# Attention, mixture of experts and feed-forward on one Trainium2 core: two-pass scores for the second pair of heads

## The chip, the core and the metric

The kernel runs on one core of a Trainium2 chip. The metric is the device time of one execution in microseconds (us), the median of several runs. PE is TensorE, ACT is ScalarE, DVE is VectorE, POOL is GpSimd, SP is SyncE, whose queue issues most of the DMAs here.

## The reference, cut to what matters

Three layers follow each other: causal attention with a bias from a cumulative sum, a top-1 mixture of experts on its output, and a feed-forward layer with a squared ReLU. The change touches the attention's scores only.

```python
batch, n_heads, seq, head_dim = (4, 8, 576, 64)      # q, k, v; s is (4, 8, 576)

scores = scale * np.matmul(q, k.transpose(0, 1, 3, 2))
causal = np.triu(np.ones((S, S), dtype=bool), k=1)
cum = np.cumsum(np.maximum(s, 0.0), axis=-1)
bias = -(cum[:, :, :, None] - cum[:, :, None, :])
scores = np.where(causal, -1000000000.0, scores + np.minimum(bias, 0.0))
...
attn = attn / (np.sum(attn, axis=-1, keepdims=True) + 1e-09)
return np.matmul(attn, v).astype(np.float32)
```

The output of all heads, as (2304, 512) rows, goes through `_moe_ref` (8 experts, 512 to 1024 to 512) and `_moe2_ref` (512 to 2048 to 512).

## The kernel before, in words

Attention works on 16 pairs of heads, pair `pp` = 0 to 15. A pair is cut into seven units of score rows (`order=[0, 1, 3, 11, 2, 10, 4]`): units 0 and 1 hold rows of both heads, 3 and 2 of the first head, 11 and 10 of the second, and 4 the last rows of both, which is called the tail. Each unit goes through the steps S (score matmuls, `emit_s`, line 636), M (mask and row minimum on DVE, line 663), E (exponential on ACT, line 680), T (transposes on PE, line 696) and V (copies out of PSUM, lines 715 and 717); later the product with v (line 733) and the transposes of the result (line 771) follow. S(1,0) below is step S of unit 0 of pair 1.

The order on every engine's queue is written out by hand. `at(key, fn, ...)` puts a step in a list, and the list is issued in the order of its keys; equal keys in the order of entry. One unit counts 1.0, so a pair counts 7, and pair `pp` has the keys around `7 * pp`. S of a pair's first unit stands at `7 * pp - 2.85`, so S(1,0) at 4.15 and S(2,0) at 11.15. An engine works through its own part of that order and waits at each instruction until its operands are there. SP's DMA issues are part of the same order.

q and k come as float32 and are split, after their transposes, in a high and a low part, each a float32r number for PE. For every pair, `qk_pe` transposes q (part 0), k (part 1) and the last 64 rows of both (part 2) on PE (lines 549 and 551) into a PSUM bank of the "t" ring, which has three banks and is shared with step T and the products with v; `qk_hi` copies the high part out on ACT (line 576), and `qk_lo` writes the low part with DVE (line 580). They go into the tiles `st_a` (three of them, used in turn) and `st_b` (two), each 128 partitions by 4 planes by 576: q high, k high, q low, k low.

The scores of a pair come in one of two forms:
- Direct, for pairs below `ND` (2 before): q of the two heads is kept in `sta` and `stb` with zeros in the other 64 partitions, and a block of scores is summed over four matmuls: q high by k high, q high by k low, q low by k high, and the bias from `cum_q` by `cum_k`.
- Packed, for the others: head 0 has both halves of `sta`, head 1 both halves of `stb`, so that one matmul contracts two products at once, and two matmuls do. This needs four more transfers, all issued by SP: `load_aug` (line 539) loads the extra rows of the bias from `aug_d` in DRAM into `stb` and `sta`; `spread_b` moves head 1's operands within the core into `stb[0:64]`, and `spread_a` moves head 0's into `sta[64:128]` (both line 584). POOL copies the other half for `stb` in `copy_b` (line 597) and clears a plane of `sta` (line 598).

`spread_b` reads `sta[64:128, 0:2]`, `copy_b` all of `sta[64:128]`; `spread_a` writes planes 0 and 3 of `sta[64:128]`. Every step whose operands overlap with an earlier one's waits for it.

The prologue (lines 1108 to 1197) builds the masks, the cumulative sums, `cum_q` and `cum_k`, writes `aug_d` (lines 1191 to 1195), and splits pair 0. `init_rest` (key 0.3, line 1206) has small DVE instructions (lines 1209 to 1218) and four small loads of the routing weights `wp` on SP (line 1221); `init_spare` (line 1225) clears tiles that take `cum_q`'s place. The loads of q and k of pair 4 have the key 3.01, v of pair 2 3.59. After attention the experts and the feed-forward layer follow on the same core.

The lines that the steps below come back to are `ND` (117), `qk_aps` (553), `move` (583), `emit_s` (609), the memsets (1161 to 1168), the products for `cum_q` (1179 to 1186), `init_spare`'s key (1236), and the keys of pair 1 (1247 to 1263).

Of the kernel before, what the change touches and what calls it, by code (L numbers as in the profile page):

```python
# [12 lines left out]
F32 = mybir.dt.float32  # L13
# [5 lines left out]
AF = mybir.ActivationFunctionType  # L19
ALU = mybir.AluOpType  # L20
# [9 lines left out]
K_ = dict(  # L30
    S=3,
    O=0,
    pbufs=4,
    NO=5,
    od=[-1.86, -0.33],
    lorder=[0, 2, 11, 10, 3, 1, 4],
    lvact=[[0], [1], [0], [1], [1], [0], [1, 0]],
    lpv=[[7.65, 7.66], [4.06, 5.56, 6.05, 6.9, 7.45]],
# [17 lines left out]
    qk=[-3.45, -2.16, -1.89],  # L56
    qkh=0.61,
    qkl=0.65,
    dup=-2.9,
    dupa=0.6,  # L60
# [22 lines left out]
    xt0=2.2,  # L83
    xt1=1.3,
    hv=0.9,
    q1=4.32,
)


# [1 line left out]
def attention_moe_ffn_kernel(  # L91
# [14 lines left out]
    nc = tc.nc  # L106
# [7 lines left out]
    SP = NB * P  # L114
    HP = H // 2
    NPAIR = B * HP
    ND = 2
    NO = K_['NO']
    MC = NT // P
    CAPS = [352, 320, 304, 304, 288, 288, 272, 256]  # L120
# [6 lines left out]
    scale = 1.0 / float(D) ** 0.5  # L127
# [89 lines left out]
    def at(key, fn, *args):  # L217
        tasks.append((key, len(tasks), fn, args))
# [232 lines left out]
    with tc.manual_schedule():  # L451
        with ExitStack() as actx:
# [16 lines left out]
            st_a = [(apool if a else apool0).tile([P, 4, S], F32R, name=f"sta{a}") for a in range(3)]  # L469
            st_b = [(apool if a else apool0).tile([P, 4, S], F32R, name=f"stb{a}") for a in range(2)]  # L470
# [15 lines left out]
            cum_q = cq_p.tile([P, 2 * ND, S], F32R, tag="cq", name="cum_q")  # L486
# [621 lines left out]
            with tc.tile_pool(name="prep", bufs=1) as prep:  # L1108
# [6 lines left out]
                cum_r = prep.tile([P, S], F32R, name="cum_r")  # L1115
                sel = prep.tile([P, 2 * ND], F32, name="sel")
# [11 lines left out]
                    out=mf, in_=zf[:, 0:P], pattern=[[-1, P]], compare_op=ALU.is_ge, fill=NEG, base=0,  # L1128
# [3 lines left out]
                    out=mt, in_=of[:, 0:P], pattern=[[1, P]], compare_op=ALU.is_gt, fill=0.0, base=0,  # L1132
# [7 lines left out]
                for hd in range(2):  # L1140
                    r = slice(64 * hd, 64 * hd + 64)
                    nc.scalar.copy(out=mask_t[r, S - TAIL:S], in_=mf[r, 64 * hd:64 * hd + 64])
                nc.vector.tensor_reduce(
                    out=sel.unsqueeze(2), in_=ident.rearrange("p (g r) -> p r g", r=NH)[:, 0:2 * ND], axis=AX.X, op=ALU.add)
                nc.vector.tensor_scalar(out=sq, in0=sq, scalar1=0.0, scalar2=None, op0=ALU.max)
                nc.vector.tensor_tensor_scan(
                    out=cum, data0=cum_r[0:NH].bitcast(F32), data1=sq, initial=0.0, op0=ALU.mult, op1=ALU.add)
# [4 lines left out]
                    out=cum_k[NH:2 * NH], in0=cum, in1=cum_k[0:NH].bitcast(F32), op=ALU.subtract)  # L1152
# [6 lines left out]
                for a in range(2):  # L1159
                    nc.gpsimd.memset(rs_t[a], 1.0)  # L1160
                for a in range(2):
                    nc.gpsimd.memset(st_b[a][0:64, 1].bitcast(F32), 0.0)
                nc.gpsimd.memset(carry, 0.0)
                nc.gpsimd.memset(carryb, 0.0)
                nc.gpsimd.memset(tbl, 0.0)
                nc.gpsimd.memset(wp, 0.0)
                nc.gpsimd.memset(st_a[1][64:128, 0:3:2].bitcast(F32), 0.0)
                nc.gpsimd.memset(st_b[1][0:64, 0:3:2].bitcast(F32), 0.0)
                load_qk(1)
                load_v(0)  # L1170
                for part in range(3):
# [5 lines left out]
                        qk_lo(0, part)  # L1177
                qk_lo(0, 2)
                for r in range(2 * ND):
                    if r < ND:  # L1180
                        nc.scalar.activation(
                            out=cum_q[:, r], in_=cum_r.bitcast(F32), func=AF.Copy, scale=sel[:, r:r + 1])
                    else:
                        nc.gpsimd.tensor_scalar(
                            out=cum_q[:, r], in0=cum_r.bitcast(F32), scalar1=sel[:, r:r + 1], scalar2=None,
                            op0=ALU.mult)
                nc.scalar.copy(out=tri, in_=mt)
                nc.scalar.copy(out=iota_r, in_=ii)
                nc.scalar.copy(out=iota8, in_=ii[:, 0:E])
# [3 lines left out]
                    out=aug_d[1, 0:2].rearrange("c r t -> (c r) t"), in_=cum_r[0:2 * NH].bitcast(F32))  # L1193
# [41 lines left out]
            NU = len(order)  # L1235
            at(NU * ND + 0.5, init_spare)

            def early(pp):
                return min(NU, 3 * max(pp - ND, 0))

            for pp in range(NPAIR):
                base = NU * pp
                t0 = base - NU
                if pp >= 2:
                    at(max(t0 + K_["ldqk"] - early(pp), t0 - 2 * NU + K_["scq"] - early(pp - 2) + 0.2), load_qk, pp)
                    at(t0 + K_["ldv"], load_v, pp)
                if pp >= 1:
                    if pp >= ND:
                        at(t0 + K_["sck"] - early(pp), scale_tail, pp, nc.gpsimd)
                    else:  # L1250
                        at(K_["od"][0], scale_tail, pp, nc.vector)
                    for part in range(3):
                        tq = t0 + K_["qk"][part] - early(pp) + (0 if pp >= ND else K_["q1"])
                        at(tq, qk_pe, pp, part)
                        at(tq + K_["qkh"], qk_hi, pp, part)
                        at(tq + K_["qkl"], qk_lo, pp, part)
                if pp >= ND:
                    tb = t0 + max(K_["dup"], K_["qk"][2] + K_["qkl"] - early(pp) + 0.4)
                    at(tb - 0.05, load_aug, pp, 1)
                    at(tb - 0.04, copy_b, pp)  # L1260
                    at(tb, spread_b, pp)
                    at(tb - K_["dup"] + K_["dupa"], spread_a, pp)
                    at(tb - K_["dup"] + K_["dupa"], load_aug, pp, 0)
                end = pp == NPAIR - 1
                units, vact, pv = (K_["l" * end + nm] for nm in ("order", "vact", "pv"))
                for i, un in enumerate(units):
                    u = base + i
                    at(u - K_["LS"], emit_s, pp, un)
                    at(u - K_["LM"], emit_m, pp, un)
                    at(u - K_["LE"], emit_e, pp, un)  # L1270
                    at(u, emit_t, pp, un)
                    at(u + K_["LV"], emit_v, pp, un, vact[i])
                for half in (1, 0) if end else (0, 1):
                    for jb, tv in enumerate(pv[half]):
                        at(base + tv, emit_pv, pp, half, [jb])
                    tv = base + pv[half][-1]
                    tx = tv + K_["xe"]
                    at(tv + K_["ov"], emit_ov, pp, half, K_["ovact"][half])
                    at(tv + K_["rc"], emit_rc, pp, half)
                    at(tv + K_["xt"], emit_xt, pp, half)  # L1280
                    if end:
                        at(tx, emit_xl, pp, half)
                    at(tx + 0.001, emit_xe, pp, half)
                    if end:
                        at(tx + 0.002, store_x, pp, *((0, 2) if half == 0 else (2, NB - 1)))
                        if half == 1:
                            at(tx + 0.002, store_x, pp, NB - 1, NB)
                if end:
                    for hd in range(2):
                        for half in range(2):  # L1290
                            at(tx + 0.003, emit_xa, pp, half, hd)
                else:
                    at(tv + K_["sx"], store_x, pp, 0, NB - 1)
                    at(tv + K_["sx"], store_x, pp, NB - 1, NB)
# [418 lines left out]
        else:  # L1713
            for i, job in enumerate(half_jobs(E + 1, "a") + half_jobs(E + 1, "b")):
                ta = 3.5 + 3.0 * i
# [108 lines left out]
```

## Time and profile before

| | us |
|---|---|
| median of 3 runs | 861.82 |
| lowest and highest | 861.45 and 862.03 |
| the profiled execution, its own time | 862.74 |
| its span, first to last instruction | 861.0 |

The profile is of one execution, taken by the hardware profiler. The span starts with the first instruction. A view by windows gives the busy time of each engine in a stretch of it, with the number of instructions in brackets, the granted TensorE clock (1.00 is 2.4 GHz, 0.50 is 1.2 GHz), the DMA engines' busy share and their rate. A timeline gives instructions in order of start, with the idle time of the engine before them in square brackets and what ended it. "PEld" is PE's weight load, which runs beside its matmuls; SPq is SP's queue, where a row is the time that issuing a DMA takes, not its transfer.

### The profile page before, as it was taken

The numbers are of one execution on the slowest core, as the hardware profiler recorded it, in microseconds if no ns is written. First come the engines' busy times: TensorE is split into PE (matmuls) and PEld (weight loads), VectorE is DVE, ScalarE is ACT, GpSimd is POOL, SyncE is SP. The second block draws the span as 40 slices with busy tenths as digits, with TensorE's granted clock in tenths as the row PEclk, the third lists the DMA queues.
The fourth block names the chain that finished last, engine by engine and source line by source line (L and its number), as shares of the span: only waits on it lengthen the run. The fifth ranks groups of instructions, "written<-read, shape, count | busy, mean of one in ns | idle before, by whom it ended". The sixth has DMA issues, their size and how long they took to land.

```text
span 861.0 us, 15161 instructions
## 1 busy us (share of the span) xinstructions
PE 843.1 (98%) x5412; PEld 748.7 (87%) x5412; DVE 520.4 (60%) x1180; ACT 452.3 (53%) x1012; POOL 262.1 (30%) x304
## 2 busy tenths in 40 slices
PE   8999999999999999999999999999999999999995
PEld 6876777777799999999999999999999999999994
DVE  7667777978777677768976767664233343232221
ACT  7787878988465446566655545443233232233221
POOL 6322334543126465566422232331101011001001
PEclk9999999999999999999999999999999999999999
DMA  7676677753287898999983433321010121001001
GB/s 168 137 162 142 144 183 180 178 127 91 78 278 232 255 252 266 233 280 274 296 246 96 147 120 101 100 84 62 13 62 37 37 75 38 1 1 37 1 0 40
DMA packets 113029, 113.14 MB, mean 131 GB/s; under 512 B 66034, under 2 KB 83954, under 8 KB 112947
## 3 DMA queue, kind: packets, MB, share of 16 engines
q1 hardware_dynamic: 104962, 96.68, 42.1%
q0 software_dynamic: 3664, 9.62, 3.3%
q10 hardware_dynamic: 4320, 5.80, 2.0%
q8 instruction: 45, 0.74, 0.4%
q14 instruction: 38, 0.30, 0.1%
HBM read 80.50 MB, written 23.32 MB: 121 GB/s over the span
## 4 chain that ended last, share of the span: by engine, by line
PE 47%; issue 31%; DVE 6%; ACT 6%; POOL 5%; DMA 4%; POOLq 1%; SPq 0%; ACTq 0%; DVEq 0%
PE z L1431 14%; PE z L1482 7%; PE z L1473 6%; PE s L636 5%; PE t L733 5%; PE t L696 4%; DMA cv<-in_moe_w_out_dram 2%; ACT p L680 2%; POOL out_dram L1541 1%; DVE w L250 1%; POOL cvm L1400 1%; PE t L549 1%; POOL cvm L1399 1%; ACT sta L576 1%; DMA w_out_d<-cvm 1%
## 5 line engine op out<-in xcount | busy, mean ns | idle before, releaser
L1431 PE MATMUL z<-xt,w 128*128 128x384 f32 (+6 forms) x1920 | 329.7, 320 | 0.7 <-DVE h L1442 0.6
L1431 PEld LDWEIGHTS z<-xt,w 128*128 128x128 f32 x1920 | 308.1, 188 | 9.8 <-DVE h L1442 1.2
L1482 PE MATMUL z<-w,h 128*128 128x512 f32 x864 | 214.9, 393 | 0.0
L1482 PEld LDWEIGHTS z<-w,h 128*128 128x128 f32 x864 | 160.7, 188 | 29.3
L1451 DVE SCALAR_TENSOR_TENSOR r<-z,r 128x384 f32<-128x384 f32 x96 | 53.3, 556 | 127.2 <-ACT r L1450 127.2
L1450 ACT ACTIVATE r<-z 128x384 f32<-128x384 f32 x96 | 47.2, 492 | 150.3 <-PE z L1431 149.3
L1473 PE MATMUL z<-h,w 128*128 128x304 f32 (+5 forms) x768 | 111.3, 294 | 0.4 <-DVE h L1442 0.2
L1473 PEld LDWEIGHTS z<-h,w 128*128 128x128 f32 x768 | 104.0, 189 | 1.2 <-ACT h L1441 0.4
L1399 POOL TENSOR_TENSOR cvm<-cvm,cva 128x512 f32<-128x512 f32 x32 | 43.5, 1361 | 170.6 <-DVE cva L1395 121.9
L1541 POOL DMA_INDIRECT out_dram<-ysb,tok_m x18 | 17.4, 969 | 245.5 <-ACT ysb L1528 183.2
L1458 DVE TENSOR_TENSOR h<-r,h 128x384 fp32r<-128x384 f32 x96 | 61.0, 636 | 50.3 <-ACT h L1457 49.7
L680 ACT ACTIVATE p<-p,nm 128x128 f32<-128x128 f32 (+3 forms) x144 | 84.3, 590 | 3.7 <-DVE nm L663 2.3
L1457 ACT CAST h<-r 128x384 fp32r<-128x384 f32 x96 | 49.3, 513 | 64.1 <-DVE r L1451 63.8
L250 DVE TENSOR_TENSOR w<-stg,w 128x1024 fp32r<-128x1024 f32 x49 | 75.1, 1534 | 5.4 <-ACT w L246 5.4
L663 DVE CUSTOM_DVE_ANT_0 p<-s,mask 128x128 f32<-128x128 f32 (+3 forms) x128 | 59.7, 486 | 30.4 <-PE s L636 29.3
L696 PE MATMUL t<-ident,p 128*128 128x128 f32 x400 | 69.1, 283 | 2.8 <-DVE sta L580 1.1
L246 ACT CAST w<-stg 128x1024 fp32r<-128x1024 f32 x49 | 51.4, 1049 | 22.0 <-POOL cvm L1400 18.2
L696 PEld LDWEIGHTS t<-ident,p 128*128 128x128 f32 x400 | 44.4, 140 | 18.7 <-ACT p L680 6.2
L597 POOL CAST stb<-sta 64x1152 fp32r<-64x1152 f32 x28 | 31.4, 1150 | 79.7 <-PE s L636 46.3
L1400 POOL TENSOR_TENSOR cvm<-cvs,cvm 128x512 f32<-128x512 f32 x32 | 54.2, 1694 | 2.5
L636 PE MATMUL s<-sta 128*64 128x288 f32 (+4 forms) x204 | 50.0, 342 | 0.9 <-DVE sta L580 0.9
L715 ACT COPY pt<-t 128x512 f32<-128x512 f32 (+1 forms) x94 | 47.0, 515 | 7.3 <-PE t L733 4.1
(242 smaller groups left out, 1024.8 us busy)
## 6 DMA issues: line engine op xcount, KB each, us to landing
stg<-in_moe_w_dram SPq DMA_DIRECT2D x42, 512.0 KB
cv<-in_moe_w_out_dram SPq DMA_DIRECT2D x16, 512.0 KB
stx<-in_moe_w_dram SPq DMA_DIRECT2D x14, 512.0 KB
cv<-in_moe_w_in_dram SPq DMA_DIRECT2D x14, 512.0 KB
xr<-yT_d SPq DMA_DIRECT2D x8, 768.0 KB
qk<-in_q_dram SPq DMA_DIRECT2D x32, 128.0 KB
v<-in_v_dram SPq DMA_DIRECT2D x32, 128.0 KB
stg<-in_moe_w_dram SPq DMA_DIRECT2D x16, 256.0 KB
```

The lines of the kernel that those rows point to most:

```text
L250: nc.vector.tensor_tensor(out=lo, in0=raw.pop(job), in1=hi.bitcast(F32), op=ALU.subtract)
L636: nc.tensor.matmul(ps[0:mw, d0:d0 + nn], lhsT=ql[r, m0:m0 + mw], rhs=kl[r, c0:c0 + nn], start=(i == 0 and (tail or n == 0)), stop=(done an ...
L663: nc.vector.tensor_tensor_reduce(out=dst, in0=src, in1=msk, scale=-1.0, scalar=3.0e38, op0=ALU.add, op1=ALU.min, accum_out=nm[:, c:c + 1])
L680: nc.scalar.activation(out=pt[:, cs], in_=pt[:, cs], func=AF.Exp, scale=-1.0, bias=nm[:, c:c + 1], accum_out=rs[:, r:r + 1])
L696: nc.tensor.transpose(tp[:, i * P:(i + 1) * P], pt[:, j0:j0 + P], ident)
L1399: nc.gpsimd.tensor_tensor(out=m, in0=m, in1=a.bitcast(F32), op=ALU.mult)
L1400: nc.gpsimd.tensor_tensor(out=m, in0=sq, in1=m, op=ALU.add)
L1431: nc.tensor.matmul(ps[:, 0:n], lhsT=wa[:, zw, kk, fl * P:(fl + 1) * P], rhs=xt[:, zx, kk, 0:n], start=(i == 0), stop=(i == 3 * KD - 1))
L1451: nc.vector.scalar_tensor_tensor(out=gg, in0=ps[:, 0:TT], scalar=0.0, in1=gg, op0=ALU.max, op1=ALU.mult)
L1458: nc.vector.tensor_tensor(out=ht[:, 1], in0=gg, in1=ht[:, 0].bitcast(F32), op=ALU.subtract)
L1473: nc.tensor.matmul(y_acc[g][d][:, 0:n], lhsT=wb[:, zw, fl, d * P:(d + 1) * P], rhs=ht[:, zh, 0:n], start=(f == 0 and i == 0), stop=(f == n ...
L1482: nc.tensor.matmul(acc, lhsT=ht[:, zh, c * P:(c + 1) * P], rhs=wb[:, zw, fl, :], start=(first and i == 0), stop=(last and i == 2))
```

## The change

`ND` goes from 2 to 1: pair 1 takes the packed form. Its transposes and copies get sooner keys (`q1` from 4.32 to 3.1): q at -0.35 instead of 0.87, k at 0.94 instead of 2.16, the last rows at 1.21 instead of 2.43, each with its high part 0.61 and its low part 0.65 behind. The steps of the packing are added for pair 1: `load_aug` for `stb` at 1.86, `copy_b` at 1.87, `spread_b` at 1.91, `spread_a` and `load_aug` for `sta` at 1.93. `cum_q` has two planes instead of four, both written by ACT; the two on POOL go. Two memsets for pair 1's direct form go, and one grows from one plane to two. `init_spare` comes at 7.5 instead of 14.5. The keys of all later pairs stay.

```diff
-    q1=4.32,
+    q1=3.1,
...
-    ND = 2
+    ND = 1
...
-                    nc.gpsimd.memset(st_b[a][0:64, 1].bitcast(F32), 0.0)
+                    nc.gpsimd.memset(st_b[a][0:64, 1:2 + a].bitcast(F32), 0.0)
...
-                nc.gpsimd.memset(st_a[1][64:128, 0:3:2].bitcast(F32), 0.0)
-                nc.gpsimd.memset(st_b[1][0:64, 0:3:2].bitcast(F32), 0.0)
...
                 for r in range(2 * ND):
-                    if r < ND:
-                        nc.scalar.activation(
-                            out=cum_q[:, r], in_=cum_r.bitcast(F32), func=AF.Copy, scale=sel[:, r:r + 1])
-                    else:
-                        nc.gpsimd.tensor_scalar(
-                            out=cum_q[:, r], in0=cum_r.bitcast(F32), scalar1=sel[:, r:r + 1], scalar2=None,
-                            op0=ALU.mult)
+                    nc.scalar.activation(
+                        out=cum_q[:, r], in_=cum_r.bitcast(F32), func=AF.Copy, scale=sel[:, r:r + 1])
...
             def early(pp):
-                return min(NU, 3 * max(pp - ND, 0))
+                return min(NU, 3 * max(pp - 2, 0))
...
-                    if pp >= ND:
+                    if pp >= 2:
                         at(t0 + K_["sck"] - early(pp), scale_tail, pp, nc.gpsimd)
...
-                        tq = t0 + K_["qk"][part] - early(pp) + (0 if pp >= ND else K_["q1"])
+                        tq = t0 + K_["qk"][part] - early(pp) + (0 if pp >= 2 else K_["q1"])
...
                 if pp >= ND:
                     tb = t0 + max(K_["dup"], K_["qk"][2] + K_["qkl"] - early(pp) + 0.4)
+                    if pp == 1:
+                        tb = K_["qk"][2] + K_["q1"] + K_["qkl"] + 0.05
                     at(tb - 0.05, load_aug, pp, 1)
                     at(tb - 0.04, copy_b, pp)
                     at(tb, spread_b, pp)
-                    at(tb - K_["dup"] + K_["dupa"], spread_a, pp)
-                    at(tb - K_["dup"] + K_["dupa"], load_aug, pp, 0)
+                    ta = tb - K_["dup"] + K_["dupa"]
+                    if pp == 1:
+                        ta = tb + 0.02
+                    at(ta, spread_a, pp)
+                    at(ta, load_aug, pp, 0)
```

## Rows read from the trace of the kernel before

**Rows 1.** Page, part 1: busy us, share of the span, instructions of each engine.
```profile
PE 843.1 (98%) x5412; PEld 748.7 (87%) x5412; DVE 520.4 (60%) x1180; ACT 452.3 (53%) x1012; POOL 262.1 (30%) x304
```

**Rows 2.** Timeline of PE: first score matmuls of pairs 1 and 2.
```profile
24.05 0.34 PE L636 MATMUL s<-sta 128*128 128x192 f32 x1
...
39.38 0.34 PE L636 MATMUL s<-sta 128*128 128x192 f32 x1
```

**Rows 3.** Windows: pair 1, pair 2, then pair 1's two halves.
```profile
24.05:39.38 15.33, 15.33 (x124) 13.21 (x122) 9.64 (x33) 10.91 (x32) 5.59 (x6) 1.00 0.72 156
39.38:52.16 12.78, 12.00 (x98) 9.68 (x96) 8.61 (x31) 10.66 (x31) 3.23 (x5) 1.00 0.73 169
...
24.05:31.35 7.30, 7.30 (x56) 6.60 (x55) 5.85 (x22) 6.50 (x21) 3.35 (x4) 1.00 0.58 132
31.35:39.38 8.03, 8.03 (x69) 6.60 (x68) 3.80 (x12) 4.41 (x13) 2.24 (x2) 1.00 0.84 178
```
The columns are the stretch, its length, then PE, PEld, DVE, ACT and POOL busy, the clock, the DMA share and GB/s.

**Rows 4.** Windows of line 636 alone: PE and PEld busy; pair 1's halves, pair 2.
```profile
24.00:31.35 7.35, 5.52 (x28) 3.99 (x28) 1.00 0.58 131
31.35:39.30 7.95, 3.38 (x21) 2.76 (x20) 1.00 0.85 179
39.30:52.10 12.80, 5.30 (x24) 3.34 (x24) 1.00 0.73 168
```

**Rows 5.** Timeline of SP's queue, pair 2's four transfers and the last of pair 3.
```profile
22.14 0.61 SPq L1221 DMA_DIRECT2D wp<-n_moe_w_output_gate_dram  x1
22.85 1.98 SPq L512 DMA_DIRECT2D qk<-in_q_dram  x2
...
29.32 0.44 SPq L539 DMA_DIRECT2D stb<-aug_d  x1
29.86 0.64 SPq L584 DMA_DIRECT2D stb<-sta  x1
...
34.73 0.62 SPq L584 DMA_DIRECT2D sta<-sta  x1
35.39 0.49 SPq L539 DMA_DIRECT2D sta<-aug_d  x1
...
46.66 0.50 SPq L539 DMA_DIRECT2D sta<-aug_d  x1
```

**Rows 6.** DMA issues of the first 60 us: one move and its size.
```profile
stb<-sta SPq DMA_DIRECT2D x3, 288.0 KB
```

**Rows 7.** Windows behind pair 2's spread_b; the last number is the DMA rate in GB/s.
```profile
30.50:31.00 0.50, 0.50 (x6) 0.50 (x4) 0.40 (x4) 0.50 (x2) 0.30 (x1) 1.00 0.08 23
31.00:32.70 1.70, 1.70 (x13) 0.87 (x13) 1.23 (x4) 1.10 (x3) 0.00 (x0) 1.00 0.91 172
```

**Rows 8.** Timelines and chain of the prologue: two loads from issue to use.
```profile
0.81 0.40 SPq L1110 DMA_DIRECT2D sq<-in_s_dram  x1
...
3.05 0.99 DVE L1145 TENSOR_SCALAR sq<-sq 32x576 f32<-32x576 f32 x1 [0.26 <-DMA sq<-in_s_dram]
...
1.73 3.99 DMA qk<-in_q_dram
```

**Rows 9.** Timeline of POOL: pair 2's copy_b and the idle time before it.
```profile
27.31 2.24 POOL L597 CAST stb<-sta 64x1152 fp32r<-64x1152 f32 x2 [6.19 <-DVE sta L580]
```

**Rows 10.** Timelines of DVE and PE: init_rest's first, q's low part, T of unit 3.
```profile
15.55 0.67 DVE L1209 TENSOR_SCALAR tok<-ij 128x20 int32<-128x20 int32 x1
...
17.31 0.42 DVE L717 COPY pt<-t 128x256 f32<-128x256 f32 x1
...
18.25 0.68 DVE L580 SCALAR_TENSOR_TENSOR sta<-t,sta 64x512 fp32r<-64x512 f32 x1
...
17.88 0.52 PE L696 MATMUL t<-ident,p 128*128 128x128 f32 x3 [0.25 <-DVE pt L717]
```

**Rows 11.** Windows behind PE's last matmuls; the clock is the third number from the end.
```profile
852.00:853.00 1.00, 0.03 (x1) 0.00 (x0) 0.00 (x0) 0.69 (x1) 0.81 (x2) 1.00 0.52 197
857.00:858.00 1.00, 0.00 (x0) 0.00 (x0) 0.00 (x0) 0.00 (x0) 0.00 (x0) 0.50 0.00 0
```

## The prediction, on record before the changed kernel ran

> **What bounds the kernel now.** I read the page's busy shares first, then the windows around the second pair's scores, then SP's queue. TensorE (PE) is busy 98% of the span, the other engines 30 to 60% [rows 1], so time is won where PE loses work and lost where it is made to wait. The stretch that the change is about runs from the first score matmul of pair 1 at 24.05 to that of pair 2 at 39.38 [rows 2]: 15.33 us, PE busy in all of it; the next pair, with two passes, takes 12.78 us with PE busy 12.00 [rows 3]. The reader should see in these rows that pair 1 is bound by PE alone, and that in its first half ACT is nearly full too (6.50 of 7.30 us).
>
> The second thing to see is SP's queue, which issues the DMAs one after another [rows 5]. The last small load of the routing weights (wp) goes out at 22.14, the q and k of pair 4 from 22.85, and so on without a gap to pair 2's four transfers: its extra rows for stb at 29.32, the move into stb (spread_b) at 29.86, the move inside sta (spread_a) at 34.73, the extra rows for sta at 35.39. Pair 2's scores begin at 39.38. An early need of pair 1 meets a queue that is full of other issues.
>
> **What is removed.** Each direct pair issues 48 score matmuls, a packed one 24. Line 636 keeps PE busy 8.89 us in pair 1's stretch (5.52 in its first half, 3.38 in its second, which add up so but for rounding) and 5.30 in pair 2's [rows 4]. So 24 matmuls are worth 8.89 - 5.30 = 3.59 us of PE time, split as the rows split: 2.23 in the first half, 1.36 in the second. The second half has ACT busy only 4.41 of 8.03 us [rows 3], so there all 1.36 count. In the first half ACT has 6.50 us of work, of which the softmax of pair 0's tail (0.78) can run ahead, while PE waits; the half can then not be shorter than some 5.7 us, which leaves 7.30 - 5.7 = 1.6 of the 2.23. I take 1.36 + 1.6 = 2.9 us, with ends 3.59 (PE alone counts) and 15.33 - 12.78 = 2.55 (pair 1 gets pair 2's period).
>
> **What is added, with one answer each.** On POOL the two products for cum_q and two memsets go, one memset doubles, and copy_b for pair 1 comes, like that of pair 2 (2.24 us) [rows 9]. POOL waited 6.19 us ahead of that one, so I cost this at nothing; without the cover copy_b would be 2.24 us later. ACT and DVE lose copies, since q's two 64-row halves become one 128-row copy: DVE has one 0.68 us instruction fewer for q's main part [rows 10], and three small ones become one. This lies in the prologue, ahead of the wait below, and I count nothing for it. init_spare's memset goes out one pair sooner, on a POOL that idles: nothing.
>
> **What is moved, and what it waits for.** Pair 1's first transposes stand at unit -0.35 now, ahead of T(0,0). The low part's subtract for q stands at 0.29999..., just ahead of init_rest at 0.3, which keeps DVE from 15.55 to the first copy behind it, some 1.7 us; before, it stood behind it [rows 10]. The three transposes of pair 1 also hold the three "t" banks longer: T of unit 3 (17.88 before, [rows 10]) now needs the bank that pair 1's k frees only when DVE has done the low part of q (0.68), init_rest (1.7), a copy, a mask step and the low part of k. I estimate that at 20.4; the work from there to pair 1's scores is as before, so PE would come to S(1,0) at about 25.8 instead of 24.05. If nothing else held S(1,0), this would cost 0 to 1.7 us.
>
> Something else does. The packed scores need both moves and both loads of extra rows. Their places are units 1.86 to 1.93, behind wp (0.3) and ahead of pair 4's q and k (3.01). So on SP load_aug comes at 22.85, where pair 4's load stood, and spread_b 0.54 us behind it as in pair 2, at 23.39 [rows 5]. spread_a overwrites sta[64:128, 0], which spread_b reads, so it has to wait until spread_b has landed; in the kernel before 4.87 us of other issues lay between the two, and no row shows that wait. It queues up SP: pair 4's q and k, pair 2's v and pair 2's own transfers stand behind it.
>
> How long a move takes, no row says directly. Pair 2's spread_b went out at 29.86, the DMA engines moved 23 GB/s until 31.00, and then 172 GB/s for 1.70 us [rows 7], some 300 KB in all, about the 288 of the move [rows 6] and its 18 of extra rows: 2.8 us from issue to landing. The nearest rows on either side are the 72 KB load of s, issued at 0.81 and used by DVE at 3.05, that is 2.24 us, and the first q load, 3.99 us in the chain that ended last [rows 8]. I take 2.8, since it is the same transfer, and keep 2.24 and 3.99 as ends.
>
> The sum: spread_b 23.39 + 2.8 = 26.2, spread_a issued there, the extra rows 0.66 later (34.73 to 35.39) at 26.9, and these land 2.24 after issue: **29.1**. S(1,0) starts there instead of 24.05, 5.05 us later. PE stands from 25.8 to 29.1, and everything behind S(1,0) in its queue stands too. Then 15.33 - 2.9 = 12.4 us to S(2,0): 41.5. The other way to S(2,0) is SP: the last of pair 1's four issues is over at 27.4, 4.55 us behind 22.85, so pair 2's last one moves from 35.39 to 39.9, or to 38.7 if two long q issues of before (1.98 and 1.54 us instead of some 1.14, [rows 5] shows the first) don't come again. It lands at 41.0 to 42.2, the same as PE's 41.5. So S(2,0) is 41.5 - 39.38 = 2.1 us later. Pair 3's last transfer went out at 46.66 [rows 5], 5.4 us before the end of pair 2's stretch, so there SP has time to spare. I carry the 2.1 us to the end unchanged.
>
> The profiled execution took 862.74 us; its span is 861.0, and the median of the runs shown is 861.82, that is 0.92 below. The sum is a difference within this one trace, so I add it to the median: 861.82 + 2.1 = **863.9 us**. Its own bounds: with legs of 2.24 S(1,0) is at 28.6 and, with 3.59 won, S(2,0) at 40.3, 1.0 late; with 3.99 it is 32.1, and with 2.55 won 44.9, 5.5 late. That is 862.8 to 867.3.
>
> The Trainium skill (DMA: Bandwidth & Descriptors, Queues, rings and completion order) says that completion on an issuing queue isn't first in, first out, so a later DMA may write before an earlier one has finished. By that rule the wait between the moves is needed, and the forecast stands; if a queue kept order, spread_a could follow at once, and the time would be that of the second case below. No run here shows it yet.
>
> **The rivals.** *Back to back* (0.20): spread_a doesn't wait for spread_b. It goes out at 24.05, the extra rows at 24.7, landing at 26.95; S(1,0) is 2.9 late and wins 2.9: 861.8, or 861.1 with 3.59. For it: nothing in the code but one overlapping slice forces the wait. Against it: the slice does overlap.
>
> *Not late at all* (0.13), the other side: the four transfers land before PE gets to S(1,0), at 24.05 to 25.8. Then 2.9 to 3.59 are won less 0 to 1.7: 858.2 to 860.6, say 859.5. The point from which it decides is SP: load_aug would have to go out by 19.5 or so for 25.8 (6.25 us lie between 22.85 and 29.1), ahead of the wp loads, and the rows put it at 22.85. For it speaks that pairs 0 and 1 are short of PE time alone, and that a gap on PE lets ACT and DVE run ahead, so some of it could come back.
>
> *The gap costs the clock, or pair 2 stalls too* (0.12): the granted clock was 1.00 (2.4 GHz) while PE's last matmuls ended at 852, and 0.50 (1.2 GHz) at 857, with PE idle between [rows 11]. If that happened in the gap before S(1,0), pair 1's packed scores (5.30 us of PE time) would take up to twice as long: up to 5.3 us more, 864 to 869, say 867. Against it: the forecast gap is shorter than that idle stretch. The Trainium skill (TensorE: Matmul & The Clock Gate, What's actually happening) says that the throttled state is the default and activity releases it. By that rule PE would come out of a long gap at the low clock; the last rows agree, none within the kernel does.
>
> *No change* (0.05): the 2.9 us and the delay cancel elsewhere, for instance in pair 2's wait of PE of 0.78 us (its 12.78 against 12.00 busy): 861.8.
>
> **How the numbers follow.** The forecast has 0.50, the rivals 0.20, 0.13, 0.12 and 0.05. The likeliest case gives 863.9, with 862.8 to 867.3 as its own range. The range over all reaches down into the third case and up to the end of the first: 860.2 to 867.4. Less than 2 in 10 is outside, most of the third case and part of the fourth. A measurement of this kernel tells 0.2% (1.72 us) from no change, so faster means under 860.1 and slower over 863.54. Faster: most of the third case, 0.12, and 0.02 of the second, 0.14. Same: the second's 0.16, the fifth's 0.05, and 0.10 of the first, whose lower end lies under the limit, 0.31. Slower: the rest, 0.55.
>
> **What would show it.** In the changed kernel S(1,0) starts near 29, with PE idle some 3 us ahead of it and the last DMA into sta as its releaser; SP shows a wait of some 2.2 us between spread_b and spread_a; line 636 is busy near 5.3 us in pair 1's stretch, and the stretch is about 12.4 us; S(2,0) starts near 41.5. I am wrong if S(1,0) starts before 27, or if the periods from pair 2 on change by more than some tenths of a us.

## The result and the profile after

The changed kernel takes **868.73 us** (median of 4 runs, 867.54 to 869.95) against 861.92 of the kernel before (4 runs, 861.45 to 862.45): ratio 1.0079, interval 1.0061 to 1.0096. It is slower, by 6.8 us, where 2.1 were forecast; the sign is right, the size is not: the time lies 1.3 us above the upper end of the range. The profiled execution took 869.95 us, its span is 868.3 (before: 861.0).

Page, part 1, of the changed kernel (against [rows 1]):
```profile
PE 840.9 (97%) x5388; PEld 746.5 (86%) x5388; DVE 519.5 (60%) x1177; ACT 451.4 (52%) x1009; POOL 260.4 (30%) x303
```
PE has 24 matmuls and 2.2 us of busy time fewer, and the span is 7.3 us longer. So PE waits somewhere for more than it saved. Its timeline says where. The timeline of PE, changed kernel, at the first scores of pairs 1 and 2 (against [rows 2]; columns: start, length, what, and in brackets the idle time before and its releaser):
```profile
23.33 0.55 PE L696 MATMUL t<-ident,p 128*128 128x128 f32 x3
31.89 0.71 PE L636 MATMUL s<-sta 128*128 128x192 f32 x2 [8.01 <-DMA sta<-aug_d]
...
46.69 0.45 PE L636 MATMUL s<-sta 128*128 128x192 f32 x2
...
211.16 0.45 PE L636 MATMUL s<-sta 128*128 128x192 f32 x2
```
PE is ready at 23.88 and gets its operands at 31.89: an idle stretch of 8.01 us, ended by the last small load into sta. S(1,0) is 7.84 us later than before, S(2,0) 7.31 later. From S(2,0) on nothing is lost or won: to the first score of the last pair it is 211.16 - 46.69 = 164.47 us here and 164.44 before (39.38 to 203.82). The whole loss lies between 23.88 and 46.69.

SP's queue, changed kernel (against [rows 5]):
```profile
21.46 1.57 SPq L1214 DMA_DIRECT2D wp<-in_moe_w_gate_dram  x1
...
23.73 0.51 SPq L539 DMA_DIRECT2D stb<-aug_d  x1
24.33 0.63 SPq L584 DMA_DIRECT2D stb<-sta  x1
27.62 0.61 SPq L584 DMA_DIRECT2D sta<-sta  x1
28.32 0.45 SPq L539 DMA_DIRECT2D sta<-aug_d  x1
...
41.21 0.48 SPq L539 DMA_DIRECT2D sta<-aug_d  x1
```
The chain is the forecast one: spread_b, a wait of SP, spread_a, the extra rows, S(1,0). Its legs are longer than forecast: 3.29 us between the two moves and 3.57 us from the last issue to S(1,0). What the DMA engines did meanwhile is seen in the DMA view of 24 to 32 us, 40 slices of 0.2 us each (busy tenths, GB/s):
```profile
DMA  1023030089999982000000005999999759967975
GB/s 10 1 15 21 3 94 0 0 196 219 207 242 196 184 173 58 0 0 0 0 0 0 0 0 127 230 196 196 184 196 184 196 141 221 236 145 165 210 170 128
```
The data of spread_b run from 25.6, 1.3 us behind its issue, to about 27.2, and spread_a goes out 0.4 us after they end. Nothing moves from 27.2 to 28.8. The data of spread_a (288 KB at some 196 GB/s are 1.5 us) run from 28.8, and the last small load, issued at 28.32, shares the engines with them and with pair 4's q behind it. The trace's chain view of this stretch gives 3.23 us from issue to landing for spread_b and 3.43 us for that load.

Windows of the changed kernel: within the idle stretch, the end of the low clock (two rows), pair 1, pair 2 (against [rows 3]; the clock is the third number from the end):
```profile
28.00:29.00 1.00, 0.00 (x0) 0.00 (x0) 0.00 (x0) 0.00 (x0) 0.00 (x0) 0.50 0.11 25
...
37.00:38.00 1.00, 1.00 (x5) 0.70 (x4) 0.03 (x1) 1.00 (x5) 1.00 (x2) 0.50 0.98 208
38.00:39.00 1.00, 1.00 (x8) 0.86 (x7) 1.00 (x4) 0.71 (x3) 0.88 (x3) 0.97 0.98 191
...
31.89:46.69 14.80, 14.80 (x96) 12.50 (x97) 8.71 (x31) 9.92 (x29) 5.04 (x7) 0.79 0.70 154
46.69:59.47 12.78, 12.00 (x99) 9.68 (x97) 8.63 (x31) 10.66 (x31) 3.86 (x5) 1.00 0.68 157
```
Window of line 636 alone, pair 1 (against [rows 4]; PE and PEld busy, then the clock):
```profile
31.80:46.60 14.80, 6.78 (x24) 4.47 (x24) 0.79 0.69 153
```
While PE idles, the clock falls from 1.00 to 0.50 (2.4 to 1.2 GHz), and it stays there until 38, with PE at work again from 31.89. The 24 score matmuls take 6.78 us instead of the 5.30 that 24 take at full clock [rows 4]. So the changed pair 1 takes 14.80 us, hardly less than the 15.33 of before.

### The profile page after: what moved, and what is told of

It is laid out like the page before. It is cut to its first block, busy times and chain, and to the rows that moved or that the text cites. A ratio compares the mean times of both kernels' runs of the same rounds, so it can differ in the third digit from the quotient of the medians.

```text
span 868.3 us, 15110 instructions
## 1 busy us (share of the span) xinstructions
PE 840.9 (97%) x5388; PEld 746.5 (86%) x5388; DVE 519.5 (60%) x1177; ACT 451.4 (52%) x1009; POOL 260.4 (30%) x303
## 4 chain that ended last, share of the span: by engine, by line
PE 50%; issue 31%; DVE 6%; ACT 5%; POOL 4%; DMA 2%; POOLq 1%; SPq 0%; ACTq 0%; DVEq 0%
PE z L1429 17%; PE z L1471 9%; PE z L1480 7%; PE t L733 4%; PE s L636 4%; PE t L696 3%; ACT p L680 2%; POOL out_dram L1539 1%; PE t L549 1%; ACT sta L576 1%; POOL cvm L1398 1%; DVE w L250 1%; PE z L333 1%; PE z L1071 1%; PE z L1099 1%
## 5 line engine op out<-in xcount | busy, mean ns | idle before, releaser
L597 POOL CAST stb<-sta 64x1152 fp32r<-64x1152 f32 x30 | 33.7, 1151 | 87.6 <-PE s L636 51.2
```

## The experiments

The theory after the result: (a) S(1,0) waits for a chain of two dependent legs, a move and then a second move with a small load behind it, and the chain starts late behind a full SP queue; (b) the idle stretch costs the clock; (c) the saved matmuls win what was forecast. Rivals: the sooner transposes themselves do the harm; or the clock would be low here anyway. Ratios are against the kernel before on the same chip.

**e1, the sooner transposes alone.** In the kernel before, with its four passes:
```diff
-    q1=4.32,
+    q1=3.1,
```


> The kernel before with q1 = 3.1 alone: pair 1 stays at four passes, its transposes and copies come 1.22 units sooner. Theory 1 (the loss is the wait of S(1,0) for the two moves and the extra rows, and the clock that falls in it): the sooner transposes cost nothing, 861.3 to 862.5 us, S(1,0) within 0.5 us of 24.05. Rival (the new order of the prologue, with the low part of q ahead of init_rest and the PSUM banks held longer, is what costs): 864 us or more, S(1,0) at 25 or later.

862.07 us, ratio 1.0012 (1.0001 to 1.0022). Timeline of PE:
```profile
23.95 0.56 PE L636 MATMUL s<-sta 128*128 128x192 f32 x3
...
39.26 0.45 PE L636 MATMUL s<-sta 128*128 128x192 f32 x2
```
S(1,0) and S(2,0) come 0.10 and 0.12 us sooner than before. That edit is harmless to the stretch; the loss comes with the packing. The median is 0.8 us above the kernel before's all the same. The last pair starts 0.08 us sooner than before (203.74), so the 0.8 us lie behind the attention part; why stays open.

**e2, the wp loads taken out of SP's way.** In the changed kernel the four wp loads of init_rest become a step of their own behind pair 1's transfers:
```diff
+            def load_wp():
...
             at(0.3, init_rest)
+            at(2.5, load_wp)
```


> The changed kernel with the four small wp loads taken out of init_rest and issued at 2.5, behind pair 1's moves. They took SP from 20.15 to 23.69 us. Theory 1: SP is the one that is late, so load_aug goes out at about 20.2 and S(1,0) starts about 3.5 us sooner, near 28.4; PE's gap is some 4.5 us instead of 8.0. If the clock falls all the same, 865.2 us; if it holds at 2.4 GHz, about 862.8. Rival (the moves wait for their operands, not for SP): S(1,0) stays near 31.9 and the time at 868.7.

866.27 us, ratio 1.005 (1.0033 to 1.0067). Timelines of SP and PE:
```profile
20.67 0.70 SPq L584 DMA_DIRECT2D stb<-sta  x1
24.46 0.62 SPq L584 DMA_DIRECT2D sta<-sta  x1
25.17 0.45 SPq L539 DMA_DIRECT2D sta<-aug_d  x1
...
28.39 0.71 PE L636 MATMUL s<-sta 128*128 128x192 f32 x2 [6.11 <-DMA sta<-aug_d]
...
44.37 0.44 PE L636 MATMUL s<-sta 128*128 128x192 f32 x2 [2.03 <-DMA sta<-aug_d]
```
The chain starts 3.66 us sooner and S(1,0) 3.50 sooner. So SP's place in time does count. But the leg between the moves is 3.79 us, the idle stretch still 6.11, the clock at 0.50 from 25 to 32. And S(2,0) wins only 2.32: it now waits itself, for pair 2's last load, which goes out at 40.56, only 0.65 us sooner than in the changed kernel, since the wp loads now stand ahead of it on SP. Soon behind that wait of 2.03 us the clock is at 0.50 once more, from 46 to 49, and the last pair starts 5.86 us later than before (209.68).

**e3, the wait between the moves taken away.** For pair 1, spread_b reads pair 0's sta, so that spread_a overwrites nothing that is still read; head 1 of pair 1 gets pair 0's operands in one half:
```diff
             def spread_b(pp):
                 a, b = st_of(pp)
+                a = st_of(0)[0] if pp == 1 else a
```


> The changed kernel, but spread_b of pair 1 reads pair 0's sta, so spread_a no longer has to wait until spread_b has landed (head 1 of pair 1 gets pair 0's operands in one half, so its scores are others; the work is the same). Theory 1: spread_a goes out right behind spread_b, at about 25.0 instead of 27.6, S(1,0) starts near 29.3 and the time falls by 2.6 us or more: 866.1 if the clock still falls, 863.7 if it holds. Rival (the landing of the last transfers is set by traffic, not by when spread_a is issued): S(1,0) within 1 us of 31.9, 868 us or more.

867.22 us, ratio 1.0056 (1.0039 to 1.0073). Timelines of SP and PE:
```profile
24.41 0.61 SPq L584 DMA_DIRECT2D sta<-sta  x1
25.12 0.74 SPq L539 DMA_DIRECT2D sta<-aug_d  x1
...
29.31 0.71 PE L637 MATMUL s<-sta 128*128 128x192 f32 x2 [5.17 <-DMA sta<-aug_d]
```
spread_a follows 0.73 us behind spread_b (issued at 23.68) instead of 3.29, so the overlapping slice is what makes SP wait. S(1,0) is 2.58 us sooner; the last load now takes 4.19 us, with 576 KB of moves ahead of it instead of 288. The stretch of 5.17 us costs the clock all the same (0.50 until about 35), and the kernel is still 6.0 us slower than the one before on this chip.

**e4, PE kept busy in the gap.** 30 matmuls on constants, into the scores' bank, ahead of S(1,0):
```diff
+            at(4.149, warm, 30, 512, "s")
```


> The changed kernel with 30 matmuls on constants (128x512, bfloat16) right ahead of S(1,0), which keep PE busy for about 6.5 of the 8.0 us that it waits. Nothing else is changed. Theory 1: the clock stays at 2.4 GHz through pair 1's stretch, S(1,0) still starts near 31.9, the stretch shrinks from 14.8 to about 12.4 us and the time falls by 2.4: about 866.3 us. Rival (the low clock costs nothing, since ACT and DVE or the transfers set the pace of the stretch): 868.7 us, the stretch still 14 us or more.

866.73 us, ratio 1.0063 (1.0046 to 1.008). Timeline of PE, and the window of pair 1:
```profile
23.76 6.64 PE L500 MATMUL s<-onesb 128*128 128x512 bf16 x30
31.72 0.44 PE L636 MATMUL s<-sta 128*128 128x192 f32 x2 [1.32 <-DMA sta<-aug_d]
...
44.30 0.44 PE L636 MATMUL s<-sta 128*128 128x192 f32 x2
```
```profile
31.72:44.30 12.58, 12.53 (x97) 9.77 (x97) 8.88 (x32) 9.88 (x30) 5.33 (x7) 1.00 0.77 169
```
S(1,0) starts where it does in the changed kernel, the clock stays at 1.00, and the stretch takes 12.58 us instead of 14.80. This separates the two parts of the loss: the low clock costs **2.2 us**, and the saved matmuls are worth 15.33 - 12.58 = **2.75 us**. The Trainium skill (TensorE: Matmul & The Clock Gate, What's actually happening) says that the throttled state is the default and activity releases it; this pair of runs agrees, 0.79 mean clock in the stretch behind an idle gap, 1.00 behind a busy one. The loss at S(2,0) then splits into 7.84 late - 2.75 won + 2.2 clock = 7.3 us. That this meets the measured 7.31 is no further test, since both terms are taken from the same 12.58; what e4 adds is the split. At the last pair e4 is 2.39 us ahead of the changed kernel (208.77 against 211.16); in the medians less shows, 5.5 us over the kernel before against 6.8, and the two intervals overlap.

**e5, pair 1's transfers on POOL's queue.** The four DMAs go out from gpsimd instead of SP, spread_b ahead of copy_b:
```diff
-                move(a[64:128, 0::3, 0:S], a[0:64, 0:2, 0:S])
+                move(a[64:128, 0::3, 0:S], a[0:64, 0:2, 0:S], nc.gpsimd if pp == 1 else nc.sync)
...
-                    at(tb, spread_b, pp)
+                    at(tb - 0.045 * (pp == 1), spread_b, pp)
```


> The changed kernel with pair 1's four transfers issued by POOL instead of SP, spread_b ahead of copy_b; all else as changed. SP's queue is then as in the kernel before. Theory (SP is late for spread_b, and a move takes 3.3 us and the last load 3.6): spread_b goes out at about 19.6 when pair 1's high parts are done, spread_a at about 23, S(1,0) starts near 27.5, PE's gap is some 3.6 us and the clock holds; then the stretch takes 12.6 us, S(2,0) starts near 40.1 and the time is about 862.3 us. Rival (transfers from POOL's queue are slower than SP's by as much as the wait that they save): S(1,0) at 30 or later, 866 us or more.

864.97 us, ratio 1.004 (1.0025 to 1.0054), between the two cases expected. Timelines of POOL and PE:
```profile
20.13 0.64 POOL L584 DMA_DIRECT2D stb<-sta  x1 [2.28 <-ACT sta L576]
...
24.64 0.59 POOL L584 DMA_DIRECT2D sta<-sta  x1 [0.95 <-DMA stb<-sta]
...
29.71 0.71 PE L636 MATMUL s<-sta 128*128 128x192 f32 x2 [5.52 <-DMA sta<-aug_d]
```
spread_b goes out 4.2 us sooner, as soon as its operands are there (its releaser is ACT's last high part). But the legs are 4.51 and 4.49 us (the last load issued at 25.22), longer than SP's 3.29 and 3.57, so S(1,0) wins 2.2 us only and the gap still costs the clock. Why POOL's legs are longer was not separated: its own copy_b runs beside the first one, and SP, which no longer waits, has its own loads under way beside both (the DMA engines move 0.91 MB from the issue of the last load to its landing, and 0.55 MB in the changed kernel).

**e6, and the transposes sooner still.** e5 with
```diff
-    q1=3.1,
+    q1=1.5,
```


> As the run with POOL's queue, and pair 1's transposes another 1.6 units sooner (q1 = 1.5), where PE, ACT and DVE have gaps. Theory (the packing loses by its wait alone; where the transfers land before PE comes to S(1,0), the 24 matmuls are won): high parts done near 15, spread_a out near 19, the last load landed near 23.5, S(1,0) starts at 24 to 25 with a gap under 1 us, the stretch takes 12.6 us, S(2,0) starts at 36.6 to 37.6, and the time is 858.5 to 860.0 us, below the kernel before. Rival (the sooner transposes push pair 0's scores back, and the packed pair gains nothing where ACT and DVE bound it): S(2,0) at 39.4 or later, 861.3 us or more.

862.64 us, ratio 1.0019 (1.001 to 1.0029), a miss for the theory. The operands now arrive in time, and another loss appears ahead of them. Timelines of DVE, POOL and PE, and two windows:
```profile
17.06 1.17 DVE L1206 TENSOR_SCALAR ik<-ij 128x20 int32<-128x20 int32 x1
18.26 1.06 DVE L1207 TENSOR_SCALAR idab<-ik 128x20 bf16<-128x20 int32 x1
...
17.05 2.24 POOL L597 CAST stb<-sta 64x1152 fp32r<-64x1152 f32 x2
...
22.05 1.12 PE L696 MATMUL t<-ident,p 128*128 128x128 f32 x4 [2.91 <-ACT p L680]
...
29.06 0.45 PE L636 MATMUL s<-sta 128*128 128x192 f32 x2
...
41.36 0.45 PE L636 MATMUL s<-sta 128*128 128x192 f32 x2
```
```profile
21.00:22.00 1.00, 0.00 (x0) 0.00 (x0) 1.00 (x5) 0.82 (x3) 0.92 (x2) 0.67 1.06 248
22.00:23.00 1.00, 0.95 (x5) 0.95 (x6) 0.36 (x4) 1.00 (x3) 0.58 (x2) 0.50 0.86 189
```
S(1,0) has no wait left, and its stretch takes 12.30 us. But copy_b on POOL now runs beside init_rest on DVE, whose two small integer instructions take 1.17 and 1.06 us (0.20 and 0.23 in the changed kernel) and end when the two copies end, at 18.2 and 19.3. init_rest keeps DVE 3.4 us, the softmax of pair 0 is late, PE stands 2.91 us, and the clock is at 0.50 until 28. The Trainium skill (SBUF — State Buffer, SBUF: two separate sides) says that GpSimd and some kinds of DVE instruction take a shared port pair as an exclusive lock for a whole instruction; the coinciding ends agree with that, but no run here shows that these two are of such a kind.

**e7, DVE's part of init_rest out of the way.** e6 with these DVE instructions as a step within pair 1:
```diff
+            def init_ids():
...
             at(0.3, init_rest)
+            at(8.9, init_ids)
```


> As the run with POOL's queue and the sooner transposes, and init_rest's small DVE instructions (token numbers, 3.4 us there beside POOL's copies) go to the key 8.9. Theory (what was left of the loss there was PE's wait for DVE at 19.1 and the clock that fell in it, not the packing): no gap over 2 us before S(1,0), the clock holds, S(1,0) starts at 24 to 25.3 when the last load lands, the stretch takes 12.6 us, S(2,0) starts at 36.6 to 37.9, 858.4 to 859.7 us, below the kernel before. Rival (a packed pair 1 gains nothing at the end even without a wait): 860.5 us or more.

861.86 us, ratio 1.0007 (0.9998 to 1.0015), again outside what the theory expected. Timelines of PE and SP:
```profile
25.64 0.44 PE L636 MATMUL s<-sta 128*128 128x192 f32 x2 [2.22 <-DMA sta<-aug_d]
...
39.43 0.44 PE L636 MATMUL s<-sta 128*128 128x192 f32 x2 [1.24 <-POOL sta L598]
...
35.80 0.49 SPq L539 DMA_DIRECT2D sta<-aug_d  x1
```
S(1,0) waits 2.22 us, the clock holds, and 25.64 + 12.3 to 12.5 would be S(2,0) at 37.9 to 38.1. It starts at 39.43, as before the change. The trace puts the wait down to a POOL memset that ran from 38.81 to 39.38, but that one is pair 3's (copy_b of pair 2 and its memset had ended at 31.3). Pair 2's last small load, issued at 35.80, is 3.63 us old at 39.43, the age that pair 1's had in the changed kernel (3.57). That points to a second bound, **SP's queue ahead of pair 2's own transfers**, which the prediction had named as the other way to S(2,0).

**e8, the same move in the kernel before.** init_ids at 8.9, four passes kept:

> The kernel before with init_rest's small DVE instructions at the key 8.9, and nothing else: what that move alone is worth. Theory: it frees DVE of 1.7 us ahead of pair 0's first copy, where PE waited 0.25 us; S(1,0) starts 0.3 to 1.5 us sooner than 24.05 and the time is 860.0 to 860.9 us. Rival (it gains as much as the packed version, so that the packing has no part in it): 859 us or less.

862.42 us, ratio 1.0014 (1.0003 to 1.0025), slower where a gain was expected. Timelines of PE and SP, and a window:
```profile
22.14 0.56 PE L636 MATMUL s<-sta 128*128 128x192 f32 x3
...
39.65 0.44 PE L636 MATMUL s<-sta 128*128 128x192 f32 x2 [1.94 <-DMA sta<-aug_d]
...
36.07 0.50 SPq L539 DMA_DIRECT2D sta<-aug_d  x1
```
```profile
41.00:42.00 1.00, 1.00 (x7) 1.00 (x6) 0.89 (x2) 0.64 (x2) 0.00 (x0) 0.50 0.24 54
```
S(1,0) is 1.91 us sooner than before, and none of it reaches S(2,0), which waits for its load 3.58 us after issue. Without any packing SP holds S(2,0) where it was. Here 1.94 us of waiting were followed by the clock at 0.50, from about 41 to 44. Pair 2's stretch takes 13.92 us (to 53.57) instead of 12.78, and the last pair starts 1.43 us later than before (205.25), about the 1.3 us by which the median is higher.

**e9, packed, with SP freed too.** e7 with the wp loads at 10.0:
```diff
+            at(10.0, load_wp)
```


> As the packed run with init_rest's DVE part at 8.9 (there S(1,0) was at 25.64, but S(2,0) at 39.43, when pair 2's own last load landed), and the four wp loads go to the key 10.0, behind pair 2's transfers. Theory (SP's queue is the second bound: pair 2's transfers land near 39.4 whatever PE does, since SP issues without a gap until then): pair 2's last load goes out 2.6 to 3.1 us sooner, near 33, S(2,0) is set by PE at 38.1 to 38.4, and the time is 1.0 to 1.3 us below the run without this, 860.0 us. Rival (the stretch of a packed pair 1 takes 13.8 us for another reason, ACT or DVE): S(2,0) stays at 39.2 or later, 861.2 us or more.

861.85 us, ratio 1.0001 (0.9991 to 1.0011). Timeline of PE:
```profile
26.52 0.71 PE L636 MATMUL s<-sta 128*128 128x192 f32 x2 [3.74 <-DMA sta<-aug_d]
...
40.22 0.45 PE L636 MATMUL s<-sta 128*128 128x192 f32 x2
```
A miss, with nothing won. S(1,0) came 0.9 us later than in e7, although its last load went out 0.54 us sooner (at 21.00, from POOL): it was used 5.52 us after its issue, and 4.10 us in e7. With wp gone SP issues its own loads sooner, and while that load was under way the DMA engines moved 1.02 MB, and 0.50 MB in e7; whether that is the cause was not tested. The gap of 3.74 us cost the clock (0.50 from about 27 to 30), and pair 2's spread_b, at 30.30, waited some 2 us for pair 2's high parts, which the gap had delayed. The test of the second bound was not clean, so the next two runs take the gap away in two ways.

**e10, direct, with SP freed.** e8 with the wp loads at 10.0, so pair 1 keeps its four passes and needs no moves:

> The kernel before, four passes for pair 1, with init_rest's DVE part at 8.9 (there S(1,0) was at 22.14 and S(2,0) at 39.65, after a wait of 1.94 us for pair 2's last load and with the clock falling behind it) and the wp loads at 10.0. Theory (as for the packed run: SP is the second bound, for the direct form too): S(2,0) is set by PE at 22.14 + 15.3 = 37.4 to 37.8, no fall of the clock, 859.2 to 859.8 us, below the kernel before and below the packed run with the same. Rival (the direct form is bound by PE's own work, and SP's queue doesn't matter to it): 861 us or more.

**859.95 us**, ratio 0.9984 (0.9974 to 0.9994, 12 runs against 23), just over the theory's upper end of 859.8. Timelines of PE and SP:
```profile
21.59 0.56 PE L636 MATMUL s<-sta 128*128 128x192 f32 x3
...
36.91 0.45 PE L636 MATMUL s<-sta 128*128 128x192 f32 x2
...
33.00 0.49 SPq L539 DMA_DIRECT2D sta<-aug_d  x1
```
Pair 2's last load goes out 2.4 us sooner than before [rows 5], and S(2,0) comes 2.47 sooner, with no wait. e8 and e10 differ in the wp loads alone, so this shows the second bound, and it is a version that beats both kernels, by 1.3 us against the one before. That is 0.16%, under the 0.2% taken as the bound for a few runs; with 12 and 23 runs the interval leaves out 1. Only part of the 2.47 arrives: the last pair starts at 202.22, 1.60 sooner than before, since pair 2's stretch now takes 13.70 us (to 50.61); why was not tested.

**e11, packed, SP freed, PE kept busy.** e9 with
```diff
+            at(4.149, warm, 10, 512, "s")
```


> The packed run with init_rest's DVE part at 8.9 and wp at 10.0 (S(1,0) at 26.52 after a gap of 3.74 us, the clock at 1.2 GHz behind it, S(2,0) at 40.22), with 10 matmuls on constants ahead of S(1,0), 2.2 us of PE time. Theory (what is left of the packed form's loss is the landing of pair 1's last load and the clock): the clock holds, S(1,0) stays at 25.6 to 26.5, the stretch is 12.4 to 12.8 us, S(2,0) at 38.0 to 39.3, and the time is 859.8 to 861.0 us, so a packed pair 1 comes to the kernel before's time or a little under, and not under the direct form with the same two moves (859.95). Rival (the packed form was held by the clock alone): S(2,0) at 36.9 or sooner, 859.2 us or less.

862.38 us, ratio 1.0009 (0.9999 to 1.002). Timeline of PE:
```profile
26.40 0.44 PE L636 MATMUL s<-sta 128*128 128x192 f32 x2 [0.96 <-DMA sta<-aug_d]
...
38.69 0.45 PE L636 MATMUL s<-sta 128*128 128x192 f32 x2
...
52.03 0.44 PE L636 MATMUL s<-sta 128*128 128x192 f32 x2 [0.32 <-DMA sta<-aug_d]
```
The clock holds, the stretch takes 12.29 us, S(2,0) is 0.69 us sooner than before, as worked out, and the time is not: by S(3,0) 0.13 is left (52.16 before), by the last pair 0.12 (203.70 against 203.82). The median is 1.1 us above the kernel before's all the same. That lies behind the attention part, in a stretch that takes 655.3 to 657.2 us from one profiled execution to another; it stays open, as in e1.

## Why the prediction was right or wrong

**The saved matmuls: right.** Forecast 2.9 us in the stretch (ends 3.59 and 2.55); e4, e6 and e11, at full clock, show 2.75, 3.03 and 3.04.

**PE ready at 25.8: wrong, without harm to S(1,0).** It was ready at 23.88. The estimate let T of unit 3 wait for a "t" bank behind init_rest; no such wait occurred, and init_rest took 1.1 us (16.23 to 17.36) instead of some 1.7. This alone did not move S(1,0), but it made the idle stretch longer by 1.9 us, and the length of that stretch is what the forecast argued from when it set the clock aside.

**The chain through SP: mechanism right, legs priced too low. This is the first step that failed.** S(1,0) came at 31.89 instead of 29.1. By terms: spread_b was issued at 24.33 instead of 23.39 (+0.94; one wp load held SP 1.57 us instead of 0.61), the first leg took 3.29 instead of 2.8 (+0.49), the step to the extra rows 0.70 instead of 0.66 (+0.04), and the last leg 3.57 instead of 2.24 (+1.33). These add up to 2.80, all of the 2.8 us. Most of it is the last leg: it took the load of s, issued to idle DMA engines, as the price of a small load that goes out 0.7 us behind a 288 KB move. In the first leg the rate of the DMA engines gave the end of the data; the time from there until the waiting issue saw it was left out (0.4 us in the changed kernel).

Both prices stood in the trace of the kernel before, which records when each transfer signals its end: pair 2's spread_b, issued at 29.86, signalled at 33.35, 3.49 us later, and its last load, issued at 35.39, at 38.85, 3.46 us later. There PE did not wait for them, so no wait showed them. In the same trace the equal load into stb, ahead of the moves, took 1.95 to 2.21 us over pairs 2 to 15, and the one into sta, behind a move, 3.1 to 4.6 us. So the long price goes with the place behind the move; how much of it is the move ahead and how much the loads behind was not separated.

**The wait between the moves: right.** SP waited, 3.29 us from issue to issue, and e3 shows that the overlapping slice makes it wait. So the rival "back to back" fell; and even with the wait gone the change would have lost, at 867.22. The rule from the Trainium skill (DMA: Bandwidth & Descriptors, Queues, rings and completion order) that completion isn't first in, first out was cited as the reason for the wait. No run here tests it: the wait is in the program, and the runs show only that it is kept.

**The clock: a rival that should have been part of the forecast. This is the second step that failed.** The sum put it at nothing, and the rival had 0.12, because the forecast gap, 3.3 us, was short. The gap was 8.01, the clock fell, and the price was 2.2 us (e4), inside the 5.3 that the rival allowed. The measured 868.73 lies within that rival's own 864 to 869, but in part by luck, since it counted no longer legs. The range failed here: its upper end, 867.4, had the longest legs without the clock, and 867 stood for the clock with the forecast legs. But long legs make the gap that costs the clock, so the two had to be added. S(1,0) itself, 31.89, lies within the bounds given for it (28.6 to 32.1; the terms give 28.5 to 32.0).

**S(2,0).** 41.5 was forecast: 2.80 for the chain, 2.2 for the clock and 0.2 for the stretch (12.58 instead of 12.4) make 46.7, the measured 46.69. SP's bound, forecast at 41.0 to 42.2, was covered by this delay (last issue at 41.21); e7, e8 and e10 show that it is real and stands next in line.

**The carry to the end: right.** 7.31 us at S(2,0), 7.34 at the last pair, 7.3 in the span, 6.8 in the median.

## What to carry to other kernels

A rearrangement through DMA is a chain of issue, data and release, and each dependent leg of it cost 3.2 to 5.7 us here, more than the 2.75 us of matmul time that it saved. Count the legs from the first moment at which the operands exist, and price a small load behind a large one by the same load in the same place, from issue to landing, and not by a load to idle engines. An idle stretch on TensorE and the low clock behind it are one event: add them up within one case. When a wait is removed, look for the next queue that sets the same start: here SP's issues held S(2,0), and e10, which takes loads with a later use out of SP's way (and a step out of DVE's), with no saved matmul at all, was the only version that came out faster.

## What the runs showed of the hardware

- An 18 KB load behind a 288 KB move was used 3.22 us (e2) to 5.70 us (e11, issued at 20.70 from POOL) after its issue, where a 72 KB load at the start took 2.24 [rows 8]. A 288 KB move within the core took 3.29 us (the changed kernel) and 3.79 us (e2) from SP's queue until what waited for it was issued, and 4.51 us (e5) to 4.70 us (e9) from POOL's.
- The clock went to 0.50 in or right behind PE waits of 8.01, 6.11, 5.52, 5.17, 3.74 and 2.91 us, and soon behind waits of 2.03 us in e2 and 1.94 us in e8; it did not behind 2.22 us in e7, 1.32 us in e4 and 0.96 in e11. The length of the wait alone does not sort these; what does was not tried.
- Two integer instructions of DVE on 128x20 elements each took about five times as long beside copies on POOL (1.17 and 1.06 us in e6 against 0.20 and 0.23 in the changed kernel).
